# Chunked attention into a gated feed-forward layer: the first k as float32 on the SP and ACT queues, a new order of loads, and small products on zeros in TensorE's early gaps

## The chip, the cores and the metric

The kernel runs on one core of a Trainium2 chip, in one launch. The metric is the device time of one execution in microseconds (us), as the median of three runs.

## The reference

q, k and v are float32 of shape (8 batches, 8 heads, 576 tokens, 64). Attention is computed within chunks of 64 tokens, so that each batch has nine chunks of their own. The result, as 4608 tokens of 512 values, goes through a layer with a Swish-like gate.

```python
scores = scale * np.matmul(q_c, k_c.transpose(0, 1, 2, 4, 3))   # per chunk of 64 x 64
scores = scores - np.max(scores, axis=-1, keepdims=True)
attn = np.exp(scores)
attn = attn / (np.sum(attn, axis=-1, keepdims=True) + 1e-09)
out = np.matmul(attn, v_c)
...
x = np.ascontiguousarray(attn_out.transpose(0, 2, 1, 3)).reshape(B * S, H * D)
h = x @ w_in                                  # 512 -> 2048
g = h * (1.0 / (1.0 + np.exp(-beta * h)))
return (g @ w_out).astype(np.float32)         # 2048 -> 512
```

## The kernel before

**Attention units.** The work on q, k and v is cut into units of chunks. Batch 0 is "wide": its units are chunks 0 to 3 (unit 0), 4 to 7 (unit 1) and chunk 8 (unit 2). Its eight full chunks are loaded with long rows, so that their tokens lie in another order in SBUF: v is sorted by products with a selection matrix (`select`, PE, tile `va`, copied to `vv`), and the output rows are sorted back by the store. All other batches have three units of three chunks each: batch 1 is units 3 to 5, batch 2 units 6 to 8, and so on.

**A unit's chain.** Each step has a tile by which the profile names it:

- VectorE (DVE) turns q and k (`turn`, tiles `qt`, `kt`); TensorE (PE) forms scores (`scores`, tile `s`, one buffer in PSUM).
- DVE takes the row maximum (`mx`) and subtracts it (`sh`); ScalarE (ACT) takes the exp (`ex`); DVE sums and inverts (`sum`, `ri`); DVE, or GpSimd (POOL) from unit 7 on, normalizes (`pn`).
- The result is transposed, by PE and an ACT copy for units 0 to 8 (`pt`, `et`), and by a DMA from SP after that; PE multiplies with v (`values`, tile `xa`); ACT, for the wide units ACT and DVE half each, writes the result into `XT` (`put`), the transposed input of the layer.

**The layer.** Tokens are taken in nine groups of 512 (j). For each of 16 slices of 128 hidden values, PE forms a sum of four products (`m_mm`, tile `hps`), ACT takes the tanh (`sg`), DVE gates (`gt`, a scalar_tensor_tensor). The first three groups are cut in two by tokens (`PIECES`): 256 and 256, 256 and 256, 320 and 192. Then each group of 128 tokens t gets its output from four times four products (`t_mm`, tile `ops`), one ACT copy (`osb`) and a store on ACT's queue. `hps`, `ops`, `va` and `pt` share four PSUM buffers, "p".

**The order.** All this is a list of tasks with an engine, an assumed length and dependencies. A planner at build time takes, again and again, the task that can start first by its model, with a penalty `pen` by kind: layer products come a little later, gates and tanh ("f") a little earlier. Every engine executes its own list in the order so found.

**The loads.** All loads that turn float32 into float16 are issued on POOL's queue in the order of `LOADS`; `PARTS` splits batch 1 into chunks 0 to 2 and 3 to 8, each with eight transfers (one per head) of q, k and v. Only the first half batch of q comes as float32, in four transfers on SP's and four on ACT's queue (`load_first`), and is cast by DVE and ACT (`cast_first`). beta follows on SP's queue. The planner holds a model of the rings that transfers occupy (`room_at`, `RING`). The framework gives each transfer one of eight semaphores in turn, for POOL's queue eight, and eight for SP and ACT together, so that a transfer is issued only when the eighth before it has landed.

Of the kernel before, what the change touches and what calls it, by code (L numbers as in the profile page):

```python
# [16 lines left out]
def kernel(  # L17
# [51 lines left out]
    small = const.tile([128, 1], FP32)  # L69
    beta_sb = const.tile([128, KG, 4], FP32)  # L70
# [45 lines left out]
    def load_last(name, b):  # L116

        f = raw_tile(name, b)[:, 2048:2304]
        t0 = 8 * CH
        for x in range(2):  # L120
            if name == "v":
                o = f[64 * x:64 * x + 64].rearrange("p (y s d) -> p y s d", y=2, s=2)
                for y in range(2):
                    nc.gpsimd.dma_start(
                        out=o[:, y],
                        in_=v[b, 4 * y + 2 * x:4 * y + 2 * x + 2, t0:t0 + CH].rearrange("s p d -> p s d"))
            else:
                nc.gpsimd.dma_start(
                    out=f[:, 128 * x:128 * x + 128],
                    in_=heads(name, b, x)[:, t0:t0 + CH, :].rearrange("r (p i) d -> r p (i d)", p=32))  # L130
# [39 lines left out]
    def make_selectors():  # L170
# [5 lines left out]
        for e in range(8):  # L176
            for y in range(2):
                nc.vector.tensor_copy(
                    out=sel[:, y, e].rearrange("p (c k) -> p c k", c=2)[:, :, 8 * e:8 * e + 8],
                    in_=diag[:, 16 * y:16 * y + 16].rearrange("p (c t) -> p c t", c=2))  # L180
# [5 lines left out]
    def turn(name, u, ss=(0, 1)):  # L186
# [3 lines left out]
        if grp is not None:  # L190
            if c0 % 4 == 0:
                f = raw[name, b][:, grp * 1024:grp * 1024 + 1024].bitcast(FP32)
                if 0 in ss:
                    tr[name, b, grp] = tr_p.tile([128, 4, 2, CH, 2], FP16, tag=name + "t", name=name + "t")
# [102 lines left out]
    def norm(u, gs, eng):  # L297
# [10 lines left out]
        else:  # L308
            pn = sm_p.tile([128, m, 2, n, CH], FP16, tag="pn", name="pn")
            for s in range(2):  # L310
                eng.tensor_tensor(  # L311
                    out=pn[:, :, s], in0=ex.rearrange("p g (c s) k -> p s g c k", s=2)[:, s],
                    in1=rb.rearrange("p g (c s) o -> p s g c o", s=2)[:, s].broadcast_to([128, m, n, CH]), op=ALU.mult)
        pr[u, gs] = pn

    def flip_pe(u, gs):
# [6 lines left out]
        f = pn.rearrange("p e g k -> p (e g k)" if grp is None else "p g s c k -> p (g s c k)")  # L323
# [48 lines left out]
    def put(u, r=None):  # L372
# [8 lines left out]
        o = XT[:, :, t0:t0 + w].rearrange("p k (c r t) -> p k c r t", c=2, r=2)[:, :, :, r]  # L381
        i = xa[u][:, r].rearrange("p (k c t) -> p k c t", k=KDM, c=2)
# [8 lines left out]
    hid, osbs = {}, {}  # L391

# [82 lines left out]
    def act(n):  # L475
# [7 lines left out]
    AHEAD, LAZY = 9999, 1.0  # L483
    TRACE = None
    LOADS = [("k", 0, 0), ("v", 0, 0), "ident", ("q", 0, 1), ("k", 0, 1), ("v", 0, 1), ("w_in", 0), ("w_in", 1),
             ("w_out", 0), ("last", "q"), ("last", "k"), ("last", "v"), ("w_out", 1), ("w_out", 2), ("w_out", 3),
             ("q", 1), ("k", 1), ("v", 1), ("q", 1, 1, 1), ("k", 1, 1, 1), ("v", 1, 1, 1)]
    PARTS = {1: [(0, 0, 3), (1, 3, 6)]}
# [14 lines left out]
    def wide(name, b, part):  # L503
        loaded[name, b, part] = pool(1.35, load_wide, name, b, part, size=512.0, rate=240.0, ring=17)

    def last(name, b):
        loaded[name, b, 2] = pool(1.25 if name != "v" else 1.6, load_last, name, b, size=128.0, rate=200.0, ring=36 if name == "v" else 17)
# [12 lines left out]
    def load_ident():  # L520
        make_identity(nc, ident)

    q_in = [task("SP", 2.2, load_first, nc.sync, "q", 0, osb_p, "osb", lag=4.3),
            task("ACT", 2.0, load_first, nc.scalar, "q", 1, osb_p, "osb", lag=4.5)]
    beta_in = task("SP", 0.5, lambda: nc.sync.dma_start(
        out=beta_sb, in_=moe_beta.rearrange("(kg p i) -> p kg i", p=128, i=4)), behind=q_in[0], lag=8.0)
    warm = task("DVE", 0.1, lambda: (nc.vector.memset(small, 0.0), nc.vector.memset(sel, 0.0)))
# [233 lines left out]
```

## Time and profile before

| | us |
|---|---|
| median of three runs | 318.81 |
| lowest, highest | 317.92, 319.35 |
| the profiled execution | 318.93 |
| its span from first to last instruction | 316.9 |
| first product of PE | 10.75 |
| first hidden product | 24.25 |
| first 128x320 product (third group of tokens) | 103.16 |
| end of the last product | 313.3 |
| mean clock granted to PE over the span | 0.989 |

The profile shows, for each engine, busy time and instructions, and the same in 40 slices of the span (tenths of a slice; 9 is 90% or more). PEclk is the share of full clock that TensorE was granted, in tenths. A row of the timeline gives start, length, engine, line, operation, output tile, input tiles and shape, then a count, and in brackets the idle time ahead of it with what ended it. A row of the waits gives who waited, for whom, the sum, how often, and the longest. L249 is line 249 of the kernel.

### The profile page before, as it was taken

Reading aid. Unit: us, or ns where it says so; the run is one execution under the profiler, and the core shown is the slowest. Engines: PE = TensorE matmul, PEld = TensorE weight load, DVE = VectorE, ACT = ScalarE, POOL = GpSimd, SP = SyncE. Lnnn points to the kernel's source line nnn. Section 1 sums busy time; section 2 is a strip of 40 time slices with the busy share of each in tenths; the row PEclk is TensorE's granted clock in tenths of the full one; section 3 lists DMA queues with packets and bytes.
Section 4 is the critical chain, followed back from the end, with each engine's and each line's share of the span. In section 5 each row is a group of like instructions: output and inputs, shape, how many; then the busy total and the mean of one; then the engine's idle time right before and its main releaser. Section 6 shows DMA issues by size and latency. Waiting matters only on the chain.

```text
span 316.9 us, 7899 instructions
## 1 busy us (share of the span) xinstructions
PE 285.8 (90%) x3254; PEld 165.0 (52%) x3254; DVE 207.3 (65%) x378; ACT 176.0 (56%) x299; POOL 161.7 (51%) x239
## 2 busy tenths in 40 slices
PE   0358787799898999999999999999999999999995
PEld 0347447376684667655455555554444444444442
DVE  3666847589898888978978888887334434334300
ACT  1337455267775777667556866667644454544511
POOL 7624389999999968899689841113000000000000
PEclk9997999999999799999999999999999999999999
DMA  6999948999999999999999963222111000001011
GB/s 100 167 212 131 204 66 71 136 137 129 175 120 155 103 63 125 165 177 131 52 199 147 134 71 85 67 64 48 43 62 41 33 33 35 33 33 68 33 66 66
DMA packets 95315, 31.54 MB, mean 100 GB/s; under 512 B 87600, under 2 KB 88880, under 8 KB 95280
## 3 DMA queue, kind: packets, MB, share of 16 engines
q0 software_dynamic: 77184, 18.12, 60.4%
q10 hardware_dynamic: 5376, 9.70, 9.1%
q1 hardware_dynamic: 12720, 3.22, 7.6%
q8 instruction: 25, 0.41, 0.6%
q14 instruction: 10, 0.08, 0.1%
HBM read 36.71 MB, written 9.44 MB: 146 GB/s over the span
## 4 chain that ended last, share of the span: by engine, by line
PE 75%; DMA 12%; POOL 7%; DVE 2%; ACT 1%; issue 1%; ACTq 0%; DVEq 0%; POOLq 0%
PE hps L399 36%; PE ops L427 35%; DMA w_out<-in_moe_w_out_dram 8%; DMA kr<-in_k_dram 3%; POOL kr L158 3%; PE s L249 3%; PE xa L353 2%; POOL qr L158 2%; POOL vr L153 2%; DVE mx L261 1%; DVE sh L270 1%; POOL w_in L163 0%; PE pt L325 0%; ACT XT L376 0%; ACT osb L437 0%
## 5 line engine op out<-in xcount | busy, mean ns | idle before, releaser
L411 ACT ACTIVATE sg<-hps,beta_sb 128x512 f32<-128x512 f32 (+3 forms) x192 | 108.5, 581 | 77.5 <-PE hps L399 74.9
L399 PE MATMUL hps<-XT,w_in 128*128 128x512 f16 (+3 forms) x768 | 145.2, 332 | 5.7 <-ACT XT L384 2.8
L417 DVE SCALAR_TENSOR_TENSOR gt<-sg,hps 128x512 f16<-128x512 f32 (+3 forms) x192 | 104.8, 551 | 69.7 <-ACT sg L411 67.9
L427 PE MATMUL ops<-w_out,gt 128*128 128x512 f16 x576 | 141.4, 379 | 0.0
L399 PEld LDWEIGHTS <-w_in 128*128 128x128 f16 x768 | 84.6, 115 | 52.7 <-issue 6.3
L427 PEld LDWEIGHTS <-gt 128*128 128x128 f16 x576 | 55.1, 98 | 59.4
L153 POOL DMA_DIRECT2D vr<-in_v_dram x64 | 45.6, 763 | 0.0
L305 POOL TENSOR_TENSOR pn<-ex,ri 128x768 f16<-128x768 f16 x17 | 25.2, 1483 | 35.2 <-ACT sg L411 15.8
L158 POOL DMA_DIRECT2D qr<-in_q_dram x64 | 38.4, 650 | 6.6 <-DMA w_out<-in_moe_w_out_dram 5.8
L158 POOL DMA_DIRECT2D kr<-in_k_dram x64 | 37.9, 623 | 1.9 <-DMA qr<-in_q_dram 1.8
L437 ACT ACTIVATE osb<-ops 128x512 f32<-128x512 f32 x36 | 21.5, 597 | 28.8 <-PE ops L427 28.4
L249 PE MATMUL s<-kt,qt 32*64 32x64 f16 x1152 | 14.6, 197 | 15.2 <-DVE kt L197 10.8
L261 DVE TENSOR_REDUCE mx<-s 128x12 f32<-128x768 f32 (+3 forms) x25 | 22.8, 914 | 7.4 <-PE s L249 7.4
L289 DVE TENSOR_REDUCE sum<-ex 128x12 f32<-128x768 f16 (+3 forms) x25 | 22.5, 901 | 4.3 <-ACT ex L278 4.2
L270 DVE TENSOR_TENSOR sh<-s,mx 128x768 f32<-128x768 f32 (+3 forms) x25 | 22.7, 911 | 0.1
L278 ACT ACTIVATE ex<-sh 128x768 f16<-128x768 f32 (+3 forms) x25 | 20.2, 814 | 2.9 <-issue 0.8
L249 PEld LDWEIGHTS <-qt 32*64 32x64 f16 x1152 | 12.1, 111 | 18.4 <-DVE qt L197 10.1
L376 ACT ACTIVATE XT<-xa 128x768 f16<-128x768 f32 (+1 forms) x22 | 17.2, 782 | 2.4 <-PE xa L353 2.0
L206 DVE STREAM_TRANSPOSE kt<-kr 128x384 f32<-128x384 f32 (+1 forms) x22 | 12.0, 544 | 4.7 <-DMA kr<-in_k_dram 2.9
L333 ACT ACTIVATE et<-pt 128x768 f16<-128x768 f16 (+3 forms) x10 | 7.3, 744 | 10.6 <-PE pt L325 10.2
L206 DVE STREAM_TRANSPOSE qt<-qr 128x384 f32<-128x384 f32 (+1 forms) x22 | 12.0, 550 | 0.4 <-DMA qr<-in_q_dram 0.4
L325 PE MATMUL pt<-ident,pn 128*128 128x128 f16 x54 | 5.3, 232 | 6.4 <-DVE pn L311 4.5
(38 smaller groups left out, 69.6 us busy)
## 6 DMA issues: line engine op xcount, KB each, us to landing
out_dram<-osb ACTq DMA_DIRECT2D x32, 256.0 KB
qr<-in_q_dram POOLq DMA_DIRECT2D x48, 72.0 KB, 4.1
kr<-in_k_dram POOLq DMA_DIRECT2D x48, 72.0 KB, 3.4
vr<-in_v_dram POOLq DMA_DIRECT2D x48, 72.0 KB, 3.3
w_in<-in_moe_w_in_dram POOLq DMA_DIRECT2D x2, 1024.0 KB, 12.4
w_out<-in_moe_w_out_dram POOLq DMA_DIRECT2D x4, 512.0 KB, 9.0
out_dram<-osb ACTq DMA_DIRECT2D x8, 128.0 KB
kr<-in_k_dram POOLq DMA_DIRECT2D x4, 128.0 KB, 7.3
```

The lines of the kernel that those rows point to most:

```text
L153: nc.gpsimd.dma_start(out=f[p:p + 64, c0:c0 + n, y, s], in_=i.rearrange("(c p) d -> p c d", p=CH))
L158: nc.gpsimd.dma_start(out=f[p:p + 32, c0:c0 + n, x], in_=i.rearrange("(c p i) d -> p c (i d)", p=32, i=2))
L206: nc.vector.transpose(out=o, in_=f.rearrange("p (e i l) -> p e i l", i=2, l=32))
L249: nc.tensor.matmul(out=x[p0:p0 + 64, r % 2, e:e + CH], lhsT=operand("q", u, r, s, h, c), rhs=operand("k", u, r, s, h, c), start=(h == 0), ...
L261: nc.vector.tensor_reduce(out=mx[:, 0:n].rearrange("p g e o -> p g (e o)"), in_=x[:, gs[0]:gs[-1] + 1, 0:E * CH].rearrange("p g (e k) -> p ...
L270: nc.vector.tensor_tensor(out=sh, in0=x[:, gs[0]:gs[-1] + 1, 0:E * CH].rearrange("p g (e k) -> p g e k", k=CH), in1=mx[:, 0:n].broadcast_t ...
L289: nc.vector.tensor_reduce(out=sm[:, 0:n * E].rearrange("p e o -> p (e o)"), in_=ex.rearrange("p g e k -> p (g e) k"), axis=AX.X, op=ALU.add)
L305: eng.tensor_tensor(out=pn.rearrange("p e g k -> p g e k"), in0=ex, in1=rb.broadcast_to([128, m, 2 * n, CH]), op=ALU.mult)
L399: nc.tensor.matmul(out=hps[:, 0:n], lhsT=w_in16[:, kg // 2, kk, kg % 2 * 512 + i:kg % 2 * 512 + 512:4], rhs=XT[:, kk, tok0:tok0 + n], star ...
L411: nc.scalar.activation(out=sg[:, 0:n], in_=hid[j, m, a][:, 0:n], func=ACTF.Tanh, scale=beta2_sb[:, kg, i:i + 1])
L417: nc.vector.scalar_tensor_tensor(out=gt_tiles[j][:, m, a:a + n], in0=hid.pop(("s", j, m, a))[:, 0:n], scalar=1.0, in1=hid.pop((j, m, a))[: ...
L427: nc.tensor.matmul(out=o, lhsT=gt_tiles[j][:, 4 * kg + i, t * 128:t * 128 + 128], rhs=w_out16[:, kg, i, :], start=(kg == 0 and i == 0), st ...
```

## The change

- The first half batch of k is loaded like that of q, as float32 in four transfers on SP's and four on ACT's queue, into two `sg` buffers, and is cast by DVE and ACT; its two transfers on POOL's queue go.
- The last chunk of batch 0 is loaded by pairs of heads: four transfers each for q, k and v instead of two, two and four.
- The order of loads changes: `w_out` 1 comes ahead, then q and k of batch 1 in whole (no `PARTS`), then `w_out` 2 and 3, then the last chunk, then v of batch 1.
- The normalized wide units are written in an order (y, r) that lets both copies into `XT` write 128 tokens in one run; the norm of a wide unit becomes two instructions for each of its halves.
- The selection of unit 0 stands behind the scores of unit 0.
- Gates and tanh get a penalty of 0.6 instead of -0.3 in the planner while attention is not more than 300 tokens ahead of the layer (`EARLY`) and fewer than 1000 are done; the planner's ring model counts four groups of DMA engines.
- Where the planner sees a gap of PE before 45 us (`WARM`), it fills it with 256-wide products on a zero tile: 41 ahead of everything, 42 ahead of the first `pt`, 10 ahead of the first `hps`, and 4 later on.

```diff
+    zero = const.tile([128, 256], FP16)
...
-    def load_last(name, b):
+    def load_last(name, b, r):
 
         f = raw_tile(name, b)[:, 2048:2304]
...
+        i = srcs[name][b, 2 * r:2 * r + 2, 8 * CH:9 * CH]
+        if name == "v":
+            p, y = 64 * (r % 2), r // 2
+            nc.gpsimd.dma_start(
+                out=f[p:p + 64].rearrange("p (y s d) -> p y s d", y=2, s=2)[:, y], in_=i.rearrange("s p d -> p s d"))
+        else:
+            nc.gpsimd.dma_start(
+                out=f[32 * r:32 * r + 32].rearrange("p (x e) -> p x e", x=2),
+                in_=i.rearrange("x (p i) d -> p x (i d)", p=32))
...
-            pn = sm_p.tile([128, m, 2, n, CH], FP16, tag="pn", name="pn")
-            for s in range(2):
-                eng.tensor_tensor(
-                    out=pn[:, :, s], in0=ex.rearrange("p g (c s) k -> p s g c k", s=2)[:, s],
-                    in1=rb.rearrange("p g (c s) o -> p s g c o", s=2)[:, s].broadcast_to([128, m, n, CH]), op=ALU.mult)
+            pn = sm_p.tile([128, m, 2, 2, 2, CH], FP16, tag="pn", name="pn")
+            for g in range(m):
+                for s in range(2):
+                    eng.tensor_tensor(
+                        out=pn[:, g, s].rearrange("p y r k -> p r y k"),
+                        in0=ex[:, g].rearrange("p (r y s) k -> p s r y k", r=2, s=2)[:, s],
+                        in1=rb[:, g].rearrange("p (r y s) o -> p s r y o", r=2, s=2)[:, s].broadcast_to([128, 2, 2, CH]),
+                        op=ALU.mult)
...
-        o = XT[:, :, t0:t0 + w].rearrange("p k (c r t) -> p k c r t", c=2, r=2)[:, :, :, r]
-        i = xa[u][:, r].rearrange("p (k c t) -> p k c t", k=KDM, c=2)
+        o = XT[:, :, t0 + 128 * r:t0 + 128 * r + 128]
+        i = xa[u][:, r].rearrange("p (k t) -> p k t", k=KDM)
...
+    def idle_mm(n):
+
+        x = ps_p.tile([128, 512], FP32, tag="p", name="idle")
+        for _ in range(n):
+            nc.tensor.matmul(
+                out=x[:, 0:256], lhsT=zero[:, 0:128], rhs=zero, start=True, stop=True)
...
-    AHEAD, LAZY = 9999, 1.0
+    AHEAD, LAZY, EARLY = 9999, 1.0, 300
+    WARM = 45.0
-    LOADS = [("k", 0, 0), ("v", 0, 0), "ident", ("q", 0, 1), ("k", 0, 1), ("v", 0, 1), ("w_in", 0), ("w_in", 1),
-             ("w_out", 0), ("last", "q"), ("last", "k"), ("last", "v"), ("w_out", 1), ("w_out", 2), ("w_out", 3),
-             ("q", 1), ("k", 1), ("v", 1), ("q", 1, 1, 1), ("k", 1, 1, 1), ("v", 1, 1, 1)]
-    PARTS = {1: [(0, 0, 3), (1, 3, 6)]}
+    HEADS = 2
+    LOADS = [("v", 0, 0), "ident", ("q", 0, 1), ("k", 0, 1), ("v", 0, 1), ("w_in", 0), ("w_in", 1),
+             ("w_out", 0), ("w_out", 1), ("q", 1), ("k", 1), ("w_out", 2), ("w_out", 3),
+             ("last", "q"), ("last", "k"), ("last", "v"), ("v", 1)]
+    PARTS = {}
...
+    first_in, chain = {}, {}
+    for eng, x, length, lag in ((nc.sync, 0, 2.2, 0), (nc.scalar, 1, 2.0, 0)):
+        e = "SP" if x == 0 else "ACT"
+        for name in "qk"[:HEADS]:
+            first_in[name, x] = chain[e] = task(
+                e, length, load_first, eng, name, x, osb_p if name == "q" else sg_p, "osb" if name == "q" else "sg",
+                lag=3.7 if name == "q" else 3.2, behind=chain.get(e))
...
+    for name in "qk"[:HEADS]:
+        cast[name, 0] = task("DVE", 0.45, cast_first, nc.vector, name, 0, after=[first_in[name, 0]])
+        cast[name, 1] = task("ACT", 0.63, cast_first, nc.scalar, name, 1, after=[first_in[name, 1], warm])
...
+        if u == 0:
+            order.append((x, selects[0]))
...
-                    pen = -0.3
+                    pen = -0.3 if done_tok - used_tok > EARLY or done_tok > 1000 else 0.6
...
+            if x["eng"] == "PE" and t < WARM and slots["p"]:
+                begin = max(free["PE"], min(slots["p"]), 4.0)
+                n = int((t - begin - 0.3) / 0.112)
+                if n > 2:
+                    idle_mm(n)
```

## The prediction

> **What bounds the kernel now.** I read the page's engines and slices first, then TensorE's timeline, then the waits of the first 130 us, then windows.
>
> ```profile
> PE 285.8 (90%) x3254; PEld 165.0 (52%) x3254; DVE 207.3 (65%) x378; ACT 176.0 (56%) x299; POOL 161.7 (51%) x239
> PE   0358787799898999999999999999999999999995
> DVE  3666847589898888978978888887334434334300
> PEclk9997999999999799999999999999999999999999
> ```
>
> TensorE (PE) is full from 104 us on. What can be won lies before: 10.75 us without a product, 16.6 us of gaps up to 104 us, and two dips of the clock. The places:
>
> ```profile
> 10.75 1.29 PE L249 MATMUL s<-kt,qt 32*64 32x64 f16 x64 [10.75 <-DVE kt L197]
> 11.98 1.89 PE L218 MATMUL va<-vr,sel 32*128 32x128 f16 x64
> 17.72 0.73 PE L325 MATMUL pt<-ident,pn 128*128 128x128 f16 x4 [3.85 <-DVE pn L311]
> 24.25 7.07 PE L399 MATMUL hps<-XT,w_in 128*128 128x256 f16 x48 [2.04 <-ACT XT L384]
> ...
> 62.65 0.58 PE L249 MATMUL s<-kt,qt 32*64 32x64 f16 x48 [1.81 <-DVE kt L206]
> ...
> 103.16 4.55 PE L399 MATMUL hps<-XT,w_in 128*128 128x320 f16 x20 [0.29 <-ACT XT L376]
> ```
>
> ```profile
> POOL vr L124 <- DMA w_in<-in_moe_w_in_dram: 8.2, 2, 4.4
> POOL qr L158 <- DMA w_out<-in_moe_w_out_dram: 5.8, 3, 2.9
> PE pt L325 <- DVE pn L311: 4.5, 3, 3.8
> DVE kt L206 <- DMA kr<-in_k_dram: 2.9, 1, 2.9
> ```
>
> GpSimd (POOL) issues nothing for 14 us, because each of its transfers waits for the eighth one before it; so batch 1 and 2 come late. VectorE (DVE) is the second bound:
>
> ```profile
> 25.00:26.00 1.00, 1.00 (x6) 0.75 (x5) 0.42 (x1) 0.75 (x2) 0.00 (x0) 0.50 1.05 207
> 90.00:100.00 10.00, 10.00 (x108) 5.94 (x106) 9.69 (x19) 5.06 (x10) 10.00 (x16) 1.00 1.45 129
> ```
>
> The third figure with a count is DVE: 9.69 of 10 us. The first row is the dip: clock 0.50, and hidden sums of four products (tanh at 25.67, 26.52, 27.38) come 0.85 us apart, 0.213 us per 256-wide product, where full clock gives 0.109.
>
> **The change, by the order of its instructions.** I follow it to one mark: the first 128x320 product (103.16 us before). The planner's new room and penalty rules cost nothing themselves; they only set this order. The fill of zero (an eighth of sel's 0.91) falls into DVE's idle time before 4.7 us. Up to the mark both kernels do the same on every engine that matters (480 score, 168 value, 256 hidden products, 64 gates), but the changed one has 104 output products behind it instead of 128. Those 24, at 0.863 us per four, come later: 5.2 us. From the mark to the last product before takes 313.34 - 103.16 = 210.2 us, with one dip (103.3 to 106.7 us) that costs 1.7. So the new end is mark + 210.2 + 5.2 - 1.7, and it is even with before at a mark of 99.7 us.
>
> *First score.* q and now k go as four transfers each on SP and on ACT. The two queues together also allow eight in flight: k's quarter r on one queue waits for q's quarter r on the other. The semaphore records give q's quarters landed by 2.70 and 3.12, 3.54 and 3.87, 4.09 and 4.26, but the last at 8.86 and 9.04. So k's last quarter goes out at 9.0 to 9.4, and behind it in ACT's queue stand the table load (1.28), a small exp (0.20) and both casts (0.63 each).
>
> ```profile
> 8.98 0.59 DVE L145 CAST qr<-osb 128x512 f16<-128x512 f32 x1 [2.16 <-DMA osb<-in_q_dram]
> 9.60 0.77 DVE L197 STREAM_TRANSPOSE qt<-qr 128x256 f32<-128x256 f32 x2
> 10.30 0.73 DVE L197 STREAM_TRANSPOSE kt<-kr 128x256 f32<-128x256 f32 x2
> ```
>
> ACT's q cast ends at 9.3 + 1.28 + 0.20 + 0.63 = 11.4. The landing of k's last quarter took from 2.0 us (q's first) to 6.8 (q's last); I take 2.8, near q's second and third (2.3 to 2.4), since the stall of 3.9 to 6.2 us is over. Then k is there at 12.1, cast by ACT at 12.7, and the first kt turn (0.40) ends at 13.2: **first score 13.2 instead of 10.75, +2.5**. Bounds: 11.3 if q's last quarter comes at 6.9 like most of its parts, 15.5 if k's takes 5 us. The Trainium skill ("DMA: Bandwidth & Descriptors", Issuing engines are not separate DMA queues) says that other issuing queues save only issue time on the same 16 engines; by that alone the first score would gain nothing, and the sum above, with its loss, agrees.
>
> *To the first hidden product (13.50 us before).* In PE's queue stand 41 products on zeros ahead of the scores and 42 between selection and first flip. The first 41 end by 10 even at 0.213 and cost nothing. The 42 start at score + 3.12 and take 4.6 us at full clock, 9.0 at half; the flip would be ready at + 6.97. So they delay it by 0.7 to 5.1; I take 1.7 (about nine of them at half clock), since the first 64 scores took 1.29 and the next 64, at 20.7, took 0.94 (the clock's records begin only at 21.4 us; I read the slow ones as half clock), and the dip at 25 us was over after one busy stretch of 3.4 us. In return the flips, selection and scores behind (3.96 us before) run at full clock: -1.3 (an estimate: 48 scores later take 0.55, where 64 took 0.94 here). The copies to XT now write runs side by side, so ACT's 0.60 no longer stands behind DVE's: -0.65. Sum -0.2: **first hidden product at 26.5**. The Trainium skill ("TensorE: Matmul & The Clock Gate", Part 1) has the clock fall to half after an idle window of about 3.4 us, which speaks against the first 41: they would be forgotten by 13.2. The row at 25 us, after 2 us of gap, agrees.
>
> *To the last gate of the first 512 tokens.* Attention of chunks 4 to 7 now stands ahead of the gates: ACT does its exp first (1.05), DVE shift (1.22), sum (1.22), reciprocal (0.25), norm (four of 0.41 instead of two of 0.68, +0.3) before any gate. Four sums fill the four PSUM buffers in 1.75 us, then PE waits 3.7 us for the flips at 26.5 + 5.5; the fifteenth sum is done at + 12.0 (before: + 7.1). Then two times four outputs (1.73), one sum (0.43), 15 sums of 0.45 (the 40-product row: 4.53 us), four outputs, one sum, tanh and gate 0.9: **49.6**. w_in, w_out and batch 1 are hidden here: batch 1 has 24 issues instead of 48 (13.8 us of POOL less), the last chunk 12 instead of 8 (2.4 more), k's two fewer (1.6), and w_out's last quarters move past q and k of batch 1. w_out's second lands near 29 (its first came at 28.3, 2.4 after w_in); the eight k issues behind it take 4.4, and 2.4 for each of the last two w_out transfers, behind q and k of batch 1 in the same rings, gives some 43 for a use at 46 or later. If that cover goes, each us late is a us.
>
> *To the mark.* Chunk 8 of batch 0 and batches 1 and 2 now follow each other without a stop. DVE has 15 full and 2 short turns, 7 row maxima and 6 each of shift, sum, reciprocal, 4 norms, their short forms, and 32 gates:
>
> ```profile
> L417 DVE SCALAR_TENSOR_TENSOR gt<-sg,hps 128x256 f16<-128x256 f32 x64 | 26.2, 418 | 7.1 <-ACT sg L411 6.2
> L261 DVE TENSOR_REDUCE mx<-s 128x12 f32<-128x768 f32 x21 | 19.8, 944 | 2.9 <-PE s L249 2.9
> ```
>
> 15 x 0.56 + 7 x 0.944 + 6 x (0.942 + 0.932 + 0.228) + 4 x 0.926 + 32 x 0.418 + 2.4 = 47.1 us, against 40.6 for PE. The waits on kr and POOL go; late next is DVE. It was 0.91 busy from 70 to 103 us (30.0 of 33); I take 0.99, as loads come 13 us of POOL's time earlier, so 47.5: **mark 97.1**. At 0.91 it is 101.4.
>
> *End.* 97.1 + 210.2 + 5.2 - 1.7 = 310.8; the last copy and store take 3.6 more: span 314.4 against 316.9. The profiled execution took 318.93, 2.0 over its span; the median of the runs is 0.1 lower. So 316.3.
>
> **Rivals.**
> 1. *The 42 products stay at half clock* (slower). PE takes its queue in order, so the flip waits to 13.2 + 3.1 + 9.0 = 25.3 instead of 21.9, and the products behind are cold too (1.3): +4.7, 321.0. For: scores and selection at 10.75 to 13.9 did not raise it in time for the second selection (1.89 again). Against: full-width products are denser work. It decides from a first flip at about 25 us. 0.15.
> 2. *DVE keeps gaps* as in 70 to 103 us: mark 101.4, 320.6. For: each score tile has one buffer, so maximum, shift and scores follow each other. Against: more units stand ready. 0.2.
> 3. *k is late*: first score 15.5, 318.6. 0.1.
> 4. *A quick front*: first score 11.3 and the clock full, -1.9 - 1.7: 312.7. For: half the software transfers beside q's last quarter. Against: ACT's queue. 0.17.
>
> My forecast keeps 0.38, 314 to 318.5.
>
> **The numbers.** Less than 0.5% (1.6 us) is about what a measurement of this kernel cannot tell from no change. Faster: rival 4 and three quarters of the forecast, 0.46. Same: the rest of it, most of 3 and half of 2, 0.27. Slower: rival 1, half of 2, the rest of 3, 0.27. Range 310.5 (rival 4 with a shorter stage to the mark) to 321.5 (rival 1).
>
> **What would show it.** First score near 13.2, ACT idle to 9 us on issuing k; 42 products from 16.3, their spacing 0.213 or 0.109; first hidden product near 26.5; a PE gap of 3 to 4 us after its sixteenth product; last gate of the second 256 tokens near 49.6; DVE over 0.95 busy from there to the mark near 97; no POOL wait on w_out that PE feels. I am wrong if k lands by 10, if the mark is beyond 100, or if PE has gaps behind it.

## The result, and the profile after

The changed kernel takes 322.92 us (median of four runs, 322.4 to 324.05) against 319.08 us for the kernel before on the same chip: a ratio of 1.0126, with a 95% interval from 1.0081 to 1.017. It is slower by 1.3%, clear of no change. The forecast was 316.3 us with a range up to 321.5, so the number and the sign were both missed. The profiled span is 320.6 us instead of 316.9.

The page of the changed kernel, engines and three rows of the slices:

```profile
PE 297.6 (93%) x3351; PEld 174.1 (54%) x3351; DVE 206.8 (65%) x382; ACT 177.3 (55%) x300; POOL 149.9 (47%) x217
PE   8196499987999999999999999999999999999995
DVE  4283777987889898988888989763433433434400
PEclk9879999997999999999999999999999999999999
```

TensorE (PE) has 97 instructions more, the products on zeros; its first slice is now full of them and its second nearly empty. GpSimd (POOL) has lost 12 us of work. The dip of the clock that stood at 103 us has moved to 75 us. TensorE's timeline at the places that the prediction named (start, length, and in brackets the idle time and what ended it):

```profile
1.09 7.21 PE L398 MATMUL idle<-zero 128*128 128x256 f16 x41 [1.09 <-DVE zero L544]
15.35 1.07 PE L247 MATMUL s<-kt,qt 32*64 32x64 f16 x64 [7.05 <-DVE kt L195]
18.18 5.64 PE L398 MATMUL idle<-zero 128*128 128x256 f16 x42
...
28.46 0.42 PE L366 MATMUL xa<-et,vv 64*64 64x64 f16 x29 [1.91 <-issue]
...
30.31 1.91 PE L407 MATMUL hps<-XT,w_in 128*128 128x256 f16 x16 [0.24 <-ACT XT L385]
35.31 0.61 PE L326 MATMUL pt<-ident,pn 128*128 128x128 f16 x8 [3.09 <-DVE gt L425]
...
70.42 0.51 PE L326 MATMUL pt<-ident,pn 128*128 128x128 f16 x6 [0.41 <-DVE pn L303]
71.83 0.38 PE L354 MATMUL xa<-et,vr 64*64 64x64 f16 x24 [0.90 <-ACT et L334]
...
74.34 0.56 PE L326 MATMUL pt<-ident,pn 128*128 128x128 f16 x6 [1.57 <-DVE gt L425]
...
103.07 0.71 PE L407 MATMUL hps<-XT,w_in 128*128 128x320 f16 x4
```

The first score is at 15.35 us where 10.75 was before and 13.2 was forecast. The first hidden product is 6.06 us later than before, at 30.31. The mark (first 128x320 product) is at 103.07, where it was before (103.16): the stage between has become 6.15 us shorter. But 24 output products are still to come, 5.2 us, and the dip no longer lies behind the mark, -1.7. That is the loss, 3.4 of the 3.7 us in span.

Why the first score is late is seen on VectorE (DVE) and ScalarE (ACT):

```profile
6.71 0.43 DVE L143 CAST qr<-osb 128x512 f16<-128x512 f32 x1 [1.22 <-DMA osb<-in_q_dram]
6.96 1.28 ACT L545 ACT_TABLE_LOAD   x1 [6.96 <-DMA osb<-in_q_dram]
...
13.86 0.43 DVE L143 CAST kr<-sg 128x512 f16<-128x512 f32 x1 [4.07 <-DMA sg<-in_k_dram]
13.87 0.63 ACT L141 ACTIVATE kr<-sg 128x512 f16<-128x512 f32 x1 [4.88 <-DMA sg<-in_k_dram]
14.53 0.77 DVE L195 STREAM_TRANSPOSE kt<-kr 128x256 f32<-128x256 f32 x2 [0.24 <-ACT kr L141]
```

Both engines stand for 4 to 5 us and wait for k alone. By the semaphore records, which tell when each part of a transfer has landed, k's quarters were issued at 2.8 to 7.0 us and landed at 9.3 to 13.8, 6.5 to 8 us after their issue. q's last quarter, which had been expected at 8.9 and 9.0, landed at 6.6 on SP's queue and at 7.0 on ACT's.

### The profile page after: what moved, and what is told of

Same layout as the page of the kernel before. It is cut to its first block, busy times and chain, and to the rows that moved or that the text cites. A ratio compares the mean times of both kernels' runs of the same rounds, so it can differ in the third digit from the quotient of the medians.

```text
span 320.6 us, 8080 instructions
## 1 busy us (share of the span) xinstructions
PE 297.6 (93%) x3351; PEld 174.1 (54%) x3351; DVE 206.8 (65%) x382; ACT 177.3 (55%) x300; POOL 149.9 (47%) x217
## 4 chain that ended last, share of the span: by engine, by line
PE 75%; POOL 8%; DMA 6%; DVE 5%; ACT 2%; issue 2%; SPq 0%; DVEq 0%; ACTq 0%; POOLq 0%
PE hps L407 34%; PE ops L435 33%; POOL vr L151 4%; POOL kr L156 3%; PE s L247 3%; DMA sg<-in_k_dram 2%; POOL qr L156 2%; PE xa L354 2%; PE idle L398 2%; DMA vr<-in_v_dram 2%; DVE gt L425 2%; DMA osb<-in_q_dram 1%; DMA qr<-in_q_dram 1%; ACT sg L419 1%; PE va L216 1%
## 5 line engine op out<-in xcount | busy, mean ns | idle before, releaser
L407 PE MATMUL hps<-XT,w_in 128*128 128x512 f16 (+3 forms) x768 | 148.4, 329 | 2.9 <-DVE gt L425 1.7
L435 PE MATMUL ops<-w_out,gt 128*128 128x512 f16 x576 | 144.7, 379 | 0.0
L407 PEld LDWEIGHTS <-w_in 128*128 128x128 f16 x768 | 83.3, 114 | 50.7 <-issue 4.9
L151 POOL DMA_DIRECT2D vr<-in_v_dram x56 | 41.4, 780 | 0.2 <-DMA kr<-in_k_dram 0.2
L156 POOL DMA_DIRECT2D qr<-in_q_dram x56 | 34.1, 641 | 14.9 <-DMA w_in<-in_moe_w_in_dram 8.6
L156 POOL DMA_DIRECT2D kr<-in_k_dram x56 | 33.7, 620 | 0.3 <-DMA qr<-in_q_dram 0.3
L398 PE MATMUL idle<-zero 128*128 128x256 f16 x97 | 14.7, 323 | 1.1 <-DVE zero L544 1.1
L398 PEld LDWEIGHTS <-zero 128*128 128x128 f16 x97 | 11.0, 116 | 4.1 <-DVE zero L544 1.1
L204 DVE STREAM_TRANSPOSE qt<-qr 128x384 f32<-128x384 f32 (+1 forms) x22 | 12.1, 552 | 0.1
## 6 DMA issues: line engine op xcount, KB each, us to landing
vr<-in_v_dram POOLq DMA_DIRECT2D x4, 128.0 KB, 10.1
```

The costliest lines, as they stand in the source:

```text
L151: nc.gpsimd.dma_start(out=f[p:p + 64, c0:c0 + n, y, s], in_=i.rearrange("(c p) d -> p c d", p=CH))
L156: nc.gpsimd.dma_start(out=f[p:p + 32, c0:c0 + n, x], in_=i.rearrange("(c p i) d -> p c (i d)", p=32, i=2))
L204: nc.vector.transpose(out=o, in_=f.rearrange("p (e i l) -> p e i l", i=2, l=32))
L398: nc.tensor.matmul(out=x[:, 0:256], lhsT=zero[:, 0:128], rhs=zero, start=True, stop=True)
L407: nc.tensor.matmul(out=hps[:, 0:n], lhsT=w_in16[:, kg // 2, kk, kg % 2 * 512 + i:kg % 2 * 512 + 512:4], rhs=XT[:, kk, tok0:tok0 + n], star ...
L435: nc.tensor.matmul(out=o, lhsT=gt_tiles[j][:, 4 * kg + i, t * 128:t * 128 + 128], rhs=w_out16[:, kg, i, :], start=(kg == 0 and i == 0), st ...
```

## The experiments

Times below are medians of 4 to 12 runs (e9 ran once); the ratio is to the kernel before on the same chip, with its 95% interval. The series ran on several chips, where the kernel before took 319.1 to 320.8 us, so a difference between medians of two series is rough to about a us. A "flip" is the transposition on TensorE (tile `pt`). "Mark, corrected" is the mark of the profiled execution, less 0.2157 us for each output product over 104 that stands ahead of it, so that all versions have the same work left. In the profiles of all versions but e11 the span is that figure plus 217.3 us (the prediction's 210.2 + 3.6 + 5.2 - 1.7) to within 0.3, 1.6 more for the kernel before, which has a dip behind its mark. So what is gained or lost, is gained or lost ahead of the mark. Three profiled executions lie well off their medians: e11's took 325.53 us, 4.0 over, and its mark is left out; e15's took 2.5 more and e8's 1.7 less than the median. The column "first score" is not alike everywhere: in e4, e6, e7, e10, e13 and e14 only 8 of the 64 products start there, and the other 56 wait for the second turn of k until 10.1 to 10.8 us; in the other versions all 64 start together.

| version | median us | ratio (95%) | first score | first hidden product | mark, corrected |
|---|---|---|---|---|---|
| before | 319.1 | 1 | 10.75 | 24.25 | 98.0 |
| after | 322.92 | 1.0126 (1.0081-1.017) | 15.35 | 30.31 | 103.1 |
| e1 k on POOL | 318.31 | 0.9962 (0.993-0.9994) | 10.51 | 26.14 | 98.7 |
| e2 no zero products | 321.86 | 1.0084 (1.0052-1.0116) | 15.09 | 28.47 | 102.5 |
| e3 gates ahead | 320.25 | 1.0031 (1.0006-1.0056) | 15.91 | 31.15 | 100.6 |
| e4 = e1 + e2 | 317.57 | 0.9952 (0.9927-0.9978) | 9.71 | 23.52 | 97.9 |
| e5 POOL held | 325.39 | 1.0166 (1.0113-1.022) | 12.99 | 30.30 | 105.6 |
| e6 = e1 + old loads | 327.72 | 1.0233 (1.0178-1.0288) | 9.82 | 25.54 | 108.6 |
| e7 = e1 + e2 + e3 | 315.44 | 0.9861 (0.982-0.9902) | 8.98 | 23.50 | 96.0 |
| e8 before + k on SP, ACT | 320.14 | 1.0021 (0.9991-1.0052) | 15.14 | 27.23 | 99.3 |
| e9 POOL held wholly | 320.9 (one run) | | 8.93 | 28.38 | 101.6 |
| e10 = e7, old copies | 315.31 | 0.9856 (0.9816-0.9896) | 9.64 | 24.07 | 96.5 |
| e11 = e7, old loads | 321.49 | 1.0051 (1.0017-1.0086) | 9.79 | 23.49 | |
| e12 = e7, selection first | 314.9 | 0.9848 (0.9808-0.9887) | 9.83 | 22.34 | 95.6 |
| e13 = e11, old last chunk | 317.57 | 0.9933 (0.9903-0.9962) | 9.07 | 23.55 | 98.4 |
| e14 = e7, old last chunk | 314.71 | 0.9856 (0.9825-0.9886) | 9.08 | 23.71 | 95.6 |
| e15 = e7, k on SP, ACT | 319.27 | 1.0004 (0.9976-1.0032) | 16.36 | 29.76 | 102.4 |
| e16 = e7, old count | 314.31 | 0.9848 (0.9816-0.9881) | 10.48 | 24.09 | 94.8 |
| e17 e12 + e14 + e16 | 312.81 | 0.977 (0.9718-0.9821) | 10.47 | 22.65 | 93.5 |

**e1: k back on GpSimd.** TensorE's order stays the same.

```
-    HEADS = 2
+    HEADS = 1
-    LOADS = [("v", 0, 0), "ident", ...
+    LOADS = [("k", 0, 0), ("v", 0, 0), "ident", ...
```

> The changed kernel with k's first four chunks back on the GpSimd queue, as its first transfer; TensorE's order of products is the same but for the count of zero products ahead of the first score (55 instead of 41). Theory A (the late first score costs one for one): first score at 10.7 to 11.2 us instead of 15.35, first hidden product near 25.7 instead of 30.3, mark near 98.5 instead of 103.1, time 322.9 - 4.6 = 318.3, that is, 0.5 to 1 us under the kernel before. Rival B (VectorE and the later loads bound the stage up to the mark in any case, so an earlier start is given back): first score as early, mark still at 101.5 or later, time 321 to 323.

```profile
10.51 0.96 PE L247 MATMUL s<-kt,qt 32*64 32x64 f16 x64 [0.89 <-DVE kt L195]
11.40 1.07 PE L216 MATMUL va<-vr,sel 32*128 32x128 f16 x64
...
23.16 0.37 PE L247 MATMUL s<-kt,qt 32*64 32x64 f16 x11 [3.87 <-issue]
...
26.14 2.05 PE L407 MATMUL hps<-XT,w_in 128*128 128x256 f16 x16
```

The first score moves by 4.8 us, the mark by 4.3 and the time by 4.6. Theory A holds: in this version a late first score is paid in full. The rows show two more things: with 0.89 us of idle time behind the zero products the selection takes 1.07 us instead of 1.89, and TensorE stops for 3.87 us in the middle of the scores with nothing in the profile that it waits for.

**e2, e4: no products on zeros.**

```
-    WARM = 45.0
+    WARM = 0.0
```

> The changed kernel without the products on zeros; the rest of TensorE's order is the same. Theory A: the 42 products between selection and first flip delay the flip by about 1.6 us and give back 1.3 us through the clock, and the first 41 are forgotten before the first score, so 322.6, no difference that is measured. Rival B (they only delay): first hidden product 1.6 us earlier, 321.3. Rival C (the early full clock is worth more than the sum had, since the chain from flips to the first hidden products is also at half clock without them): first hidden product 0.5 to 1.5 us later, 323.5 to 324.5.

> The changed kernel with k's first chunks back on the GpSimd queue and without products on zeros. Theory A: the sum of the two edits alone, first score near 10.8, time 318.3 - 0.3 = 318.0. Rival B: with an early first score the zero products are worth more, since only 2 to 3 us of idle time are then between the first group of them and the first score, so that the scores and selections of the other version run at full clock: this one 1 to 2 us slower than that, 319.3 to 320.3.

e2 against the changed kernel, the same places:

```profile
21.82 0.73 PE L326 MATMUL pt<-ident,pn 128*128 128x128 f16 x4 [3.85 <-DVE pn L310]
...
28.47 2.38 PE L407 MATMUL hps<-XT,w_in 128*128 128x256 f16 x16 [1.98 <-ACT XT L385]
33.47 1.01 PE L326 MATMUL pt<-ident,pn 128*128 128x128 f16 x8 [2.61 <-DVE gt L425]
34.27 2.60 PE L407 MATMUL hps<-XT,w_in 128*128 128x256 f16 x12
```

From first score to first hidden product it takes 13.38 us without them and 14.96 with them; at the mark 0.6 us of that is left, since twelve hidden products take 2.60 us at half clock here and 1.47 there. The time is 1.1 us lower in e2 and 0.7 in e4, less than the intervals separate. e2 lies between its theory A (322.6) and its rival B (321.3), its rival C is out, and rival B of e4 falls. All six kernels with products on zeros (after, e1, e3, e5, e6, e9) show a stop of TensorE of 1.38 to 3.87 us "issue" between 19 and 30 us, and none of the thirteen others does. In all six a 16 KB transfer on the instruction queue ends 1.2 to 1.4 us before TensorE goes on (it runs from 26.20 to 27.16 us in the changed kernel, from 20.65 to 21.80 in e1). The thirteen others have such a transfer between 20 and 30 us too, without a stop. That the stop waits for it is argued, not shown.

**e3, e7: gates and tanh always ahead.**

```
-    AHEAD, LAZY, EARLY = 9999, 1.0, 300
+    AHEAD, LAZY, EARLY = 9999, 1.0, -9999
```

> The changed kernel with the planner's old rule that gates and tanh always go ahead (a penalty of -0.3 at any time); 120 instead of 104 output products now stand before the mark. Theory A (the order between first hidden product and mark hardly matters, as both kernels' stages are equal to 1 us once the 24 products are counted): mark 103.1 + 16 x 0.2157 = 106.5, time 322.9 within 1 us. Rival B (holding gates back costs: the first 512 tokens' last gate moves from 54.9 to about 51): time 320 to 321.5. Rival C (it frees the attention chain): time 324 or more.

> The changed kernel with three edits: k's first chunks back on the GpSimd queue, no products on zeros, gates and tanh always ahead. Theory A (the three costs add): 317.6 - 2.7 = 314.9. Rival B (the stage up to the mark is bound by VectorE's work, so that the earlier gates give nothing once the front is early): 316.8 to 318.

The planner's hold on gates costs 2.7 us (after to e3) and 2.1 us (e4 to e7), and the intervals of the ratios are apart in both pairs. Theory A of e3, which had the order as free, falls and its rival B holds; in e7 the costs nearly add (314.9 expected, 315.44 measured). In e3 the stretch that is at 70 to 76 us in the changed kernel reads:

```profile
71.22 0.51 PE L326 MATMUL pt<-ident,pn 128*128 128x128 f16 x6 [0.44 <-DVE pn L303]
71.56 1.04 PE L407 MATMUL hps<-XT,w_in 128*128 128x256 f16 x8
72.80 5.88 PE L407 MATMUL hps<-XT,w_in 128*128 128x256 f16 x44 [0.20 <-DVE gt L425]
```

Three gaps (0.41, 0.90 and 1.57 us) have shrunk to 0.64 together, and the clock does not dip. In the changed kernel the gates stood on VectorE behind a sum, a reciprocal, a normalisation and two turns:

```profile
70.41 0.95 DVE L287 TENSOR_REDUCE sum<-ex 128x12 f32<-128x768 f16 x1
...
72.27 0.92 DVE L303 TENSOR_TENSOR pn<-ex,ri 128x768 f16<-128x768 f16 x1
73.11 0.41 DVE L425 SCALAR_TENSOR_TENSOR gt<-sg,hps 128x256 f16<-128x256 f32 x1
73.44 0.57 DVE L204 STREAM_TRANSPOSE kt<-kr 128x384 f32<-128x384 f32 x1
73.93 0.71 DVE L425 SCALAR_TENSOR_TENSOR gt<-sg,hps 128x256 f16<-128x256 f32 x2
```

After these 2.9 us without products the clock was at half for 3.4 us, from 74.64. e4 shows the same dip (69.19 to 72.60), e7 none.

**e5, e9: who makes k late.** GpSimd copies a column of each half of k, and so waits until k has landed: in e5 behind its two transfers of v's first chunks, in e9 ahead of all its transfers.

```
+            nc.gpsimd.tensor_copy(out=hold_sb[:, x:x + 1], in_=kept["k", x][:, 0:1])
 e5: LOADS = [("v", 0, 0), "ident", "hold", ("q", 0, 1), ...
 e9: LOADS = ["ident", "hold", ("v", 0, 0), ("q", 0, 1), ...
```

> The changed kernel, but GpSimd issues nothing behind v's first four chunks until both halves of k on the SP and ACT queues have landed (two GpSimd copies of one column each read them). Theory A (k took 6.5 to 8 us from issue to landing because the transfers that GpSimd issues between 4 and 12 us use the same DMA engines): k has landed by 10 us, first score at 11 to 12 instead of 15.35; the held transfers come 4 to 6 us later, so the first hidden product is at 28 to 31 and the time 320 to 323. Rival B (the landing is long for a reason of the two queues themselves, since a transfer there waits for the eighth before it): k lands at 12 or later as now, first score still 14.5 or later, time 324 or more.

> As the version that held GpSimd's transfers until k had landed, but v's first four chunks are held too, so that q and k on the SP and ACT queues have the DMA engines to themselves; the rest of the kernel starts late and its time is not of interest. Theory A (k's quarters take 6 us because software transfers share the engines): k's last quarter lands by 9.5 us and each takes 2 to 3 us, as q's first ones did. Rival B (sixteen transfers on two queues are slow by themselves): the last lands after 11 us, with 5 us and more from issue to landing.

e9, all engines:

```profile
6.99 0.61 ACT L143 ACTIVATE kr<-sg 128x512 f16<-128x512 f32 x1
7.12 0.77 DVE L197 STREAM_TRANSPOSE qt<-qr 128x256 f32<-128x256 f32 x2 [1.87 <-ACT qr L143]
...
7.82 0.39 DVE L145 CAST kr<-sg 128x512 f16<-128x512 f32 x1
...
8.93 0.70 PE L249 MATMUL s<-kt,qt 32*64 32x64 f16 x64 [1.03 <-DVE kt L197]
```

With the DMA engines to themselves k's quarters land at 5.5 to 7.0 us, 2.1 to 2.6 us after their issue, and the first score is at 8.93, earlier than before. Beside v's first chunks alone (e5) the last lands at 11.6, and beside all of GpSimd's transfers at 13.8. So the landing time is set by what else moves; e9's theory A holds, and e5 lies between its two. In e5 the price is only moved: w_in and everything behind it comes later, and by the medians the kernel is 2.5 us slower than the changed one, within the intervals. e9 was 2 us faster than the changed kernel although v's first transfer went out 6.7 us later; it ran once, without an interval.

**e6, e11, e13, e14: the loads.** e6 is e1 and e11 is e7 with the old order and parts; e13 and e14 load the last chunk of batch 0 by the old halves, at the place that it has in e11 and in e7.

```
 e13, e14 (load_last itself is the old one too):
-        for r in range(4):
-            loaded[name, b, 2] = pool(
-                0.5, load_last, name, b, r, ...
+        loaded[name, b, 2] = pool(1.25 if name != "v" else 1.6, load_last, name, b, ...
 e6, e11:
-             ("w_out", 0), ("w_out", 1), ("q", 1), ("k", 1), ("w_out", 2), ("w_out", 3),
-             ("last", "q"), ("last", "k"), ("last", "v"), ("v", 1)]
-    PARTS = {}
+             ("w_out", 0), ("last", "q"), ("last", "k"), ("last", "v"), ("w_out", 1), ("w_out", 2), ("w_out", 3),
+             ("q", 1), ("k", 1), ("v", 1), ("q", 1, 1, 1), ("k", 1, 1, 1), ("v", 1, 1, 1)]
+    PARTS = {1: [(0, 0, 3), (1, 3, 6)]}
```

> The version with k on the GpSimd queue and zero products (318.3 us), with the loads of batch 1 and of the last chunk in the old order and parts (24 more issues on GpSimd before batch 2); the planner writes out another order from 40 us on, with 112 output products before the mark instead of 104. Theory A (batch 1 earlier is worth the 4 us of the earlier mark): VectorE waits for k of batch 1 again, time 320.5 to 322.5. Rival B (the loads are hidden either way and VectorE bounds the stage): 318 to 319.

> The fastest version so far (315.4 us) with the old order and parts of the loads; 128 output products then stand before the mark, as in the kernel before. Theory A (the new loads are what that version gains on the kernel before): 318.5 to 320. Rival B (the late loads cost 9 us only where gates are held back, and little here): 315.5 to 317.

> The version with the old loads, k on the GpSimd queue, no zero products and gates ahead (321.5 us), with the last chunk of batch 0 loaded by the old halves (2, 2 and 4 transfers instead of 4, 4 and 4) at the same places; TensorE's order is the same. Against the kernel before only the planner's count of finished tokens and the chunk order are then left. Theory A (the four transfers more on GpSimd, ahead of w_out's second quarter, delay all of batch 1 and cost the 2.4 us): 319 to 320. Rival B (the planner's count, which moves scores and flips of batch 1 and 2 behind hidden products, costs them): 321 to 322.

> The version with k on the GpSimd queue, no zero products and gates ahead (315.4 us), with the last chunk loaded by the old halves; TensorE's order is the same. In this order of loads the last chunk stands behind w_out and q and k of batch 1, so theory A has it at the same time within 0.5 us; rival B (the transfers land earlier or later by more than chunk 8's turns can wait) at 316.5 or more, or at 314.5 or less.

The new order is worth 6.0 us with the last chunk by head pairs (e11 to e7), more than theory A had, and 9.4 us where gates are held back (e6 to e1; e6 is 5 us above its own theory A). But the last chunk by head pairs costs 3.9 us in the old place (e11 against e13; e13 came in below both of its theories) and 0.7 in the new (e7 against e14, inside the interval). So most of the 6.0 undoes a cost that the head pairs bring themselves: with the old halves the new order is worth 2.9 us (e13 to e14), and the changed loads as a whole 2.1 us against the loads of the kernel before (e13 to e7). GpSimd's issues in the timeline show what the head pairs do in the old place. First e11:

```profile
31.45 1.67 POOL L166 DMA_DIRECT2D w_out<-in_moe_w_out_dram  x3
...
39.72 0.56 POOL L156 DMA_DIRECT2D qr<-in_q_dram  x1 [3.86 <-DMA w_out<-in_moe_w_out_dram]
42.15 0.56 POOL L156 DMA_DIRECT2D qr<-in_q_dram  x1 [1.87 <-DMA w_out<-in_moe_w_out_dram]
44.72 0.56 POOL L156 DMA_DIRECT2D qr<-in_q_dram  x1 [2.01 <-DMA w_out<-in_moe_w_out_dram]
45.28 4.43 POOL L156 DMA_DIRECT2D kr<-in_k_dram  x8
```

The same issues in e13:

```profile
29.08 1.68 POOL L169 DMA_DIRECT2D w_out<-in_moe_w_out_dram  x3
...
34.52 0.56 POOL L159 DMA_DIRECT2D qr<-in_q_dram  x1 [0.99 <-DMA w_out<-in_moe_w_out_dram]
37.94 0.56 POOL L159 DMA_DIRECT2D qr<-in_q_dram  x1 [2.86 <-DMA w_out<-in_moe_w_out_dram]
40.46 0.56 POOL L159 DMA_DIRECT2D qr<-in_q_dram  x1 [1.97 <-DMA w_out<-in_moe_w_out_dram]
41.02 4.43 POOL L159 DMA_DIRECT2D kr<-in_k_dram  x8
```

Each transfer on GpSimd waits for the eighth ahead of it to land. Four small transfers more stand ahead of w_out's second quarter, which goes out at 31.45 instead of 29.08; the three waits for w_out behind it add up to 7.7 us instead of 5.8, and k of batch 1 goes out at 45.28 instead of 41.02. A part of this may belong to e11's long execution: in e6, which has the same loads, k of batch 1 goes out at 43.88.

**e8, e15: the price of k's way elsewhere.** e8 is the kernel before with k on SP and ACT, e15 is e7 with HEADS = 2.

```
 e8:
+    k_in = [task("SP", 2.2, load_first, nc.sync, "k", 0, sg_p, "sg", lag=3.7, behind=q_in[0]),
+            task("ACT", 2.0, load_first, nc.scalar, "k", 1, sg_p, "sg", lag=3.7, behind=q_in[1])]
-    LOADS = [("k", 0, 0), ("v", 0, 0), "ident", ...
+    LOADS = ["gap", ("v", 0, 0), "ident", ...       (gap: planned as the old transfer, issues nothing)
```

> The kernel before with one part of the change: k's first four chunks on the SP and ACT queues as float32, behind q, and cast on VectorE and ScalarE. TensorE's order is kept but for the second selection, which stands ahead of the first flip. Theory A (the front costs one for one here too): first score near 15, mark near 107.4, time 319.1 + 4.3 = 323.4. Rival B (the gaps between the first hidden product and the mark, which wait for GpSimd's loads, take the delay up): first score as late, mark at 105 or earlier, time 321 or less.

> The changed kernel with gates always ahead and no zero products, k on the SP and ACT queues as changed; against the version of 315.4 us only k's way differs, with the same order on TensorE. Theory A (with early loads the stage to the mark is one chain, so a late first score costs one for one): 315.4 + 4.4 = 319.8. Rival B (with gates ahead the stage takes up a part, as it does in the kernel before): 317 to 318.5.

In e15 it costs 3.8 us by the medians, near theory A. In e8 the first score is as late (15.14), and the time is only 0.8 us higher (319.3 for the kernel before in that series), not told from zero; its rival B holds. A part of that is e8's own: its order has the second selection in the wait for the first flip, and score to hidden product takes 12.1 us instead of 13.5. In the profiled execution another 1.7 us went into the gaps that the kernel before has ahead of its mark, and the dip behind the mark did not occur; as this execution took 1.7 us less than e8's median, the missing dip need not be the rule. So the same edit has a price of 1 to 2 us (2 when e8's own 1.4 is added) or of some 4; that this is by what the other edits have taken out behind it is the likely reading, not tested by itself.

**e10: old copies.** The normalisation, selectors and copies to XT of the kernel before, in e7.

```
...
-        o = XT[:, :, t0 + 128 * r:t0 + 128 * r + 128]
...
+        o = XT[:, :, t0:t0 + w].rearrange("p k (c r t) -> p k c r t", c=2, r=2)[:, :, :, r]
```

> The fastest version so far (k on the GpSimd queue, no zero products, gates always ahead; 315.4 us) with one more part undone: the old order of chunks in the normalisation, the selectors and the strided copies to XT. TensorE's order is the same. Theory A (ScalarE's copy waits for VectorE's in both layouts, and the layout is worth nothing on the path): 315.0 to 316.0. Rival B (contiguous copies are worth their 0.65 us at each of two places): 316.5 to 317.

Theory A holds: contiguous copies are worth nothing here. VectorE's copy takes 0.69 us and ScalarE's 0.60 in both, and ScalarE's waits for VectorE's in both.

**e12, e16, e17: towards a better version.**

```
 e12:
+            if u == 1:
+                order.append((x, first_flip[0]))
 e16:
-            if x["fn"] is put and x["args"][-1] != 1:
+            if x["fn"] is put:
```

> The fastest version so far (315.4 us) with the second selection ahead of the first flip in TensorE's queue, where TensorE otherwise waits 3.85 us for VectorE. Theory A (the 1.9 us of the selection leave the path to the first hidden product and the mark follows one for one): first hidden product near 21.8 instead of 23.5, time 313.7. Rival B (w_in's first half lands at 21.2, and VectorE or the second half of w_in bounds what follows): 314.8 to 315.6. Rival C (v's second four chunks land late and hold up the first flip): 316 to 317.

> The version of 315.4 us with the old count in the planner (each finished group of four chunks counted twice), which moves output and hidden products ahead of attention from 50 us on; 128 instead of 120 output products before the mark. Theory A (the count is the lost 2.4 us): 313 to 314. Rival B (both orders are equal within what is measured, as the same work is done up to the mark): 315 to 316. Rival C (the old count starves VectorE of scores): 317 or more.

> The edits that the runs showed as gains, together: k on the GpSimd queue, no zero products, gates ahead, the second selection ahead of the first flip, the last chunk in its old halves, the old count of finished tokens. Theory A (they add): 314.3 - 0.5 - 0.7 = 313.1. Rival B (the three small ones share one slack and only one counts): 314.3 to 315.

e16 undoes one more edit of the change, which the list of the change does not name: the planner counts each finished group of four chunks once, where the kernel before counted it twice. e12 and e16 alone are 0.5 and 1.1 us under e7, inside the intervals; e12 is as its rival B had it, and e16 lies between its theories A and B. In e12 the second selection itself waits 2.98 us for v; the first hidden product comes 1.2 us earlier than in e7, of which 0.4 is left at the mark. Together with e14 they are 2.6 us under e7, at 312.81 us, and 2.3% under the kernel before (1.8 to 2.8%). e17 is the fastest version of all. The sum of its three edits (313.1 expected) fits, but e7 and e17 ran on different chips, the intervals of their ratios just touch, and none of the three is settled by itself.

## Why the prediction was wrong

The chain from the kernel before to the changed one, by the medians: the planner's count and ring model, the chunk order and the place of unit 0's selection -1.8 (before to e13), the last chunk by head pairs and the new order of loads -2.1 together (+3.9 to e11, -6.0 to e7), gates held +2.1 (e4), zero products +0.7 (e1, inside the intervals), k on SP and ACT +4.6 (after). Which edit gives the first -1.8 stays open: undone in e7, neither the count (e16) nor the chunk order (e10) makes the kernel slower. So the change holds gains of 3.9 us together, of which the prediction saw the part of the loads, and two large losses: of k's it saw half, of the held gates' nothing.

- **First score, 13.2 forecast, 15.35 measured: the failed term is the landing of k's last quarter, 2.8 us taken and 6.7 to 7.1 measured** (issued at 6.62 and 7.02, there at 13.8). The prediction had the bounds, 2.0 to 6.8, and chose by q's second and third quarters, which were there by 4.3 us, while GpSimd's packets begin only at 3.2. The near row was q's last one, 6.8 us beside GpSimd's transfers. e9 and e5 show that this is what decides. That q's last quarter would hold k up until 9 was wrong the other way (it landed at 6.6 and 7.0) and saved nothing, as k's took longer still. Rival 3, "k is late", had the first score right (15.5) and had been given 0.1; its time, 318.6, was 4.3 us short, as the terms below were off too.
- **The first score counts one for one**: right in this kernel (e1: 4.8 us of score, 4.6 of time), but not in every kernel (e8: 4.4 of score, 0.8 of time, or some 2 with its own 1.4).
- **The 42 products delay the flip by 1.7**: right, about 1.6. Rival 1 did not occur: full clock came at 20.0, so some nine of them ran at half, as taken. **The clock gives back 1.3**: about 1.9 (flip to first hidden product takes 6.65 us in e2 and in the changed kernel, whose 6.65 hold the stop of 1.91). **ScalarE's copies run beside VectorE's, -0.65**: wrong; ScalarE still waits for VectorE's copy (row below), and the layout is worth nothing (e10). **Not in the sum: the stop of 1.9 us** in the value products (row at 28.46). Together 14.96 us to the first hidden product instead of 13.3.

```profile
29.67 0.60 ACT L385 ACTIVATE XT<-xa 128x512 f16<-128x512 f32 x1 [2.83 <-DVE XT L387]
```

- **The first 41 products cost nothing and are forgotten**: right. The clock's records begin at 6.4 us with full clock (12 products in 4 to 6 us, 18 in 6 to 8, below; the clock column shows 1.00 ahead of the first record too), and from 13.2 us it was half, 4.9 us after the last of them. The Trainium skill ("TensorE: Matmul & The Clock Gate", Part 1) has the clock fall after an idle window of about 3.4 us, and these 4.9 us, which are longer than one such window, do not speak against it. The prediction's own row at 25 us does not bear that rule out, though it says so: there the clock fell at 24.79 after a gap of only 2.04 us.

```profile
4.00:6.00 2.00, 2.00 (x12) 1.39 (x10) 1.45 (x18) 0.00 (x0) 2.00 (x4) 1.00 0.81 93
6.00:8.00 2.00, 2.00 (x18) 1.72 (x17) 0.43 (x1) 1.04 (x1) 1.40 (x3) 1.00 1.01 134
```

- **Last gate of the first 512 tokens, 23.1 us later**: 24.5. The gap of 3.7 us was 3.09; from 45.8 us on the hidden sums came three at a time, 0.54 us each instead of 0.45. That only three buffers were left for them is argued, not shown.
- **The stage to the mark, 47.5 us with VectorE 0.99 busy**: it took 48.2, but for other reasons. Windows of the changed kernel, where the third figure with a count is VectorE:

```profile
54.85:70.00 15.15, 15.05 (x258) 7.78 (x256) 13.70 (x26) 6.42 (x11) 14.48 (x24) 1.00 1.42 158
70.00:78.10 8.10, 5.22 (x101) 4.02 (x101) 6.32 (x13) 4.53 (x9) 7.87 (x13) 0.79 1.59 133
78.10:103.07 24.97, 23.97 (x350) 17.64 (x348) 22.07 (x46) 19.07 (x37) 20.08 (x31) 1.00 1.14 115
```

VectorE is busy for 42.1 us, not 47.1, and 0.87 of the time, which is less than rival 2 had. Two errors cancelled. The 47.1 was a sum of mean durations, and records of neighbouring instructions overlap: a maximum that starts at 62.17 and takes 0.96 is followed by a sum at 63.05. The durations of VectorE's records in this stretch do add up to 46.5. The idle time was put at 0.5 us, and was 6.1. TensorE's own 44.2 us of work, 1.7 of them the dip, is nearer to a bound; 2.9 of its 4.0 idle us are in the middle row, with the three gaps ahead of the dip. e3 takes gaps and dip away and gains 2.7 us. So the second step that failed is a term put at nothing: the prediction had the planner's new penalty rule as free, since it only sets the order, and it is the second loss.
- **The end from the mark**: right. 103.07 + 217.3 = 320.4 against a span of 320.6, and it holds in the other profiles.
- **Loads 13 us of GpSimd earlier**: right in kind: 2.1 us against the old loads (e13 to e7), which the losses hid. **w_out hidden behind q and k of batch 1**: right, TensorE waits for it nowhere in the changed kernel.
- **The issuing queue**: the prediction cited the Trainium skill ("DMA: Bandwidth & Descriptors", Issuing engines are not separate DMA queues), that other issuing queues save only issue time. The runs agree: 2.1 to 2.6 us alone, 6.5 to 8 beside the others. It spoke against this part of the change, and the prediction weighed it as a side remark.

## What to carry to other kernels

A transfer's time is that of its neighbours: take its duration from a row that runs beside the same traffic, and of two bounds the one whose surroundings match, not the one nearest in kind. What an early delay costs depends on the slack behind it, so an edit that removes slack can raise the price of another one (as e8 against e15 suggest for k's way); e7, which is the change without three of its edits, is 3.9 us faster than the kernel before, and these three turn it into a loss of 3.8. And a sum of mean durations is no busy time where records overlap: compare it with the busy time of a window first. An edit undone in one place can also be worth something else in another: the head pairs cost 3.9 us in the old order of loads and nothing measurable in the new.

## What the runs showed of the hardware

- 64 KB transfers on SP's and ACT's queues landed 2.1 to 2.6 us after issue alone (e9), 6.5 to 8 us beside the transfers that GpSimd issued (128 KB each, and w_in from 9.1 us on; after).
- Products on zeros do raise the granted clock: full from 6.4 us, 5.3 us after the first of them, where the record without them (e2) begins with full clock at 26.3 us. All six kernels that have them also show a stop of TensorE of 1.4 to 3.9 us with no releaser in the profile; the kernels without them have none. Why is open.
- Three gaps of 0.41, 0.90 and 1.57 us within 4.3 us stood ahead of a dip of the clock of 3.4 us; with 0.64 us of gaps in that place (e3) there was none. A single gap of 2.04 us stood ahead of the dip at 24.79 in the kernel before, while the stop of 1.91 us in the changed kernel brought none.
